# Shifted copies of attention values moved from DMA to VectorE, a split transpose and a gated load

## The chip, the cores and the metric

The kernel runs on one core of a Trainium2 chip. The metric is the device time of one execution in microseconds (us). The engines are TensorE (PE, with its weight loads shown apart as PEld), VectorE (DVE), ScalarE (ACT), GpSimd (POOL) and SyncE (SP); each runs its own instructions in order, and they wait for one another by semaphores. DMAs are issued here from GpSimd's queue and from SyncE's.

## The reference

Eight batches of causal sliding-window attention with eight heads of 576 rows and 64 columns, followed by a two-layer network with SiLU on the 4608 rows of 512 that come out.

```python
rel = pos[:, None] - pos[None, :]
mask_plain = (rel >= 0) & (rel < 32)                         # heads 0 to 3
mask_dil = (rel >= 0) & (rel < 128) & (rel % 4 == 0)         # heads 4 to 7
scores = where(mask, q @ k.T / 8, -1e9)
attn_out = softmax(scores) @ v
x = attn_out.transpose(0, 2, 1, 3).reshape(4608, 512)
h = x @ w_in                                                 # 512 -> 2048
out = (h * sigmoid(h)) @ w_out                               # 2048 -> 512
```

## The kernel before

**The main loop.** For each batch `b`, layer one makes sixteen blocks `h` of 128 hidden features (L700, 8 matmuls with 288 columns each; batch 0 in halves at L720), and ScalarE writes SiLU of them to `gT` (L708). Layer two (L765; batch 0 at L739) multiplies four row tiles of 128 in an even batch and five in an odd one, sixteen matmuls of 512 columns to a tile; `store` copies a finished tile to `ob` (L749, mostly VectorE) and writes it out from SyncE (L750).

**The attention of later batches is laid between.** `plan_of(b)` is a schedule by hand: `at(step, function, ...)` puts a function ahead of a step. Steps 0 to 15 are the sixteen blocks of layer one, and from step 16 on each step is four matmuls of layer two. What stands first in a step is issued first; nothing reorders the instructions of an engine afterwards. `z` is 0 for the four plain heads and 1 for the four dilated ones. `scores` (L371 plain, L383 dilated) are small matmuls, then VectorE adds the mask and takes row maxima (L495, L504, L511), ScalarE takes exponentials (`exps`, L534 and L543), VectorE normalises (`normal`, L552 to L559, writes `pn`), `pn` is turned to `ptT` by TensorE (`turn`, L568, with copies L576) or from batch 2's schedule on by a DMA on SyncE (`turn_by_dma`, L583), and `values` (L610, L674) multiplies with the values, and VectorE and ScalarE copy the result to `xT` (`finish`, L679 to L687).

**The values and their shifted copies.** A query block of 32 rows needs 64 rows of keys and values. `load_v` brings a batch's values from DRAM by six DMAs on GpSimd's queue into `vw`, of which there are two (batch `b` uses `vws[b % 2]`): most go to partitions 64 to 127, blocks of 64 rows. Blocks that start 32 rows later are made from these by four copies inside `vw` to partitions 0 to 63: `shift_class` (L202, 32 partitions x 2048 elements), `shift_over` (L207, 32x1024) and `shift_plain` (L195, 32x2304, and L197, 32x4x512); `shift_v` calls all of them. The argument `copy` says who does it: `nc.sync.dma_start`, `nc.gpsimd.dma_start` or `dve`, which is `nc.vector.tensor_copy`. For batches 2 and 3 the copies are DMAs in GpSimd's queue, for batches 1 and 4 to 7 DMAs in SyncE's; parts of batch 0's are made by VectorE.

**Queries and keys.** From batch 3 on, `load_rows` (L133 for plain heads, L140 for dilated) brings keys, then queries, to `nat` by twelve DMAs on GpSimd's queue, and `cross` turns them on SyncE: `z == 0` by one DMA transpose of 64 partitions x 5120 columns into `plain`, keys in the first half and queries in the second (L150), `z == 1` by two into `strided` (L155, L156). `scores` read `plain` and `strided`.

**What sets the order around the change.** GpSimd's and SyncE's queues are in order, so a DMA that waits for its data holds up all behind it. Before batch 3's `load_v`, GpSimd's queue holds batch 2's four shift DMAs, which wait for batch 2's values to land. In the schedules of `b` = 2 to 5, SyncE's queue holds the four shift DMAs of batch `b + 2` ahead of the two `cross`. A DMA on GpSimd's queue also waits for the one eight ahead of it, since eight semaphores take turns.

Of the kernel before, what the change touches and what calls it, by code (L numbers as in the profile page):

```python
# [8 lines left out]
F16 = mybir.dt.float16  # L9
# [6 lines left out]
P = 128  # L16
W = 32
# [8 lines left out]
RT = 64  # L26
# [3 lines left out]
def kernel(  # L30
# [9 lines left out]
    nc = tc.nc  # L40
    B, H, S, D = q.shape
# [7 lines left out]
    NM = NB // 2  # L49
# [11 lines left out]
    cpool = ctx.enter_context(tc.tile_pool(name="const", bufs=1))  # L61
# [19 lines left out]

    ZR = S // RT + 1
    ZC = W + CL + TL
    natural = [cpool.tile([P, 4 * ZR * P + 2 * HH * DIL * D], F16, name=f"nat{i}") for i in range(2)]
    plain = [cpool.tile([P, W + 4 * ZR * RT], F16, name=f"plain{i}") for i in range(2)]
    strided = [cpool.tile([P, W + 4 * HH * ZC], F16, name=f"strided{i}") for i in range(2)]
    kTs, qTs = [
        [t[:, o : o + 2 * ZR * RT].rearrange("p (i c) -> p i c", i=2)[:, :, 0:n] for t in plain]  # L90
        for o, n in ((0, W + S), (W + 2 * ZR * RT, S))
    ]
# [5 lines left out]
    def natural_of(n, which):  # L98
        o = which * (2 * ZR * P + HH * DIL * D)
        return natural[n % 2][:, o : o + H * 7 * D].rearrange("p (u d) -> p u d", d=D)  # L100
# [21 lines left out]
    def load_rows(b, zs=(0, 1)):  # L122

        n = natural[(b + 1) % 2]
        o = 4 * ZR * P
        f = n[0:RT, 0:o].rearrange("p (x m h d) -> p x m h d", x=4, h=2, d=D)
# [18 lines left out]
    def cross(b, z):  # L145

        n = natural[(b + 1) % 2]
        o, w = 4 * ZR * P, 2 * HH * DIL * D
        if z == 0:
            nc.sync.dma_start_transpose(  # L150
                out=plain[b % 2][:, W:].rearrange("d (g p) -> d g p", p=RT), in_=n[0:RT, 0:o]
            )
        else:
            t = strided[b % 2][:, W:].rearrange("d (g c) -> d g c", c=ZC)
            nc.sync.dma_start_transpose(out=t[:, :, 0:P], in_=n[:, o : o + w])  # L155
            nc.sync.dma_start_transpose(out=t[:, :, P:CL], in_=n[RT : RT + CL - P, 0:w])  # L156
# [82 lines left out]
    def clear_v(b, engine):  # L239
# [13 lines left out]
        out=band[0:W], in_=band[0:W], compare_op=ALU.is_ge, fill=NEG,  # L253
# [3 lines left out]
        out=band[0:W], in_=band[0:W], compare_op=ALU.is_ge, fill=NEG,  # L257
# [471 lines left out]
    dve, act = both = (nc.vector.tensor_copy, nc.scalar.copy)  # L729
# [48 lines left out]
    def transposes(at, b, z, step):  # L778
        for which in (1, 0):
            at(step, transpose, b, z, which, both)  # L780

    def later(at, b, z, steps, copies=(nc.vector.tensor_copy, nc.vector.tensor_copy)):

        for hi in (0, 1):
            if steps[hi] is not None:
                at(steps[hi], normal, b, z, hi)
        for hi in (0, 1):
            at(steps[2], turn, b, z, hi)
        for hi in (0, 1):
            at(steps[2], turned, b, z, hi, copies[hi])  # L790
        at(steps[3], values, b, z)
        at(steps[3], finish, b, z, copies)

    def plan_of(b):
        ev = {}

        def at(s, fn, *args):
            ev.setdefault(s, []).append((fn, args))

        def all_exps(b, z):  # L800
            for hi in (0, 1):
                at(16, exps, b, z, hi)

        if b == 0:

            at(-16, normal, 0, 1, 1)
            at(-15, shift_class, 0, dve, 1, 2)
            at(-14, normal, 0, 0, 1)
            at(-13, clear_v, 1, nc.vector)
            at(-13, load_v, 1)  # L810
            for c in (2, 3):
                at(-13, load_w_out, c)
            at(-13, load_qk, 2)
            at(-8, turn, 0, 1, 1)
            at(-8, turned, 0, 1, 1, act)
            at(-6, values0, 1, 1)
            at(-6, last_values, 0, 1, (1,))
            at(-6, finish0, 1, 1)
            at(-6, last_finish, 0, 1, 1)
            at(-4, turn, 0, 0, 1)  # L820
            at(-4, turned, 0, 0, 1)
            at(-2, values0, 0, 1)
            at(-2, last_values, 0, 0, (1,))
            at(-2, finish0, 0, 1, both)
            at(-2, last_finish, 0, 0, 1)
            transposes(at, 1, 1, 2)
            at(8, scores, 1, 1)
            for hi in (0, 1):
                at(8, shift, 1, 1, hi)
            for which in (1, 0):  # L830
                at(17, transpose, 1, 0, which, (dve, dve))
            at(20, normal, 1, 1, 0)
            at(20, scores, 1, 0)
            at(14, shift_v, 1, nc.sync.dma_start)
            at(17, load_rows, 3)
            at(17, load_v, 2)
            at(17, shift_v, 2, nc.gpsimd.dma_start)
            all_exps(1, 1)
            for hi in (0, 1):
                at(20, exps, 1, 0, hi)  # L840
            for n, z, hi in ((20, 1, 1), (26, 0, 0), (28, 0, 1)):
                at(n, normal, 1, z, hi)
            for n, z, copies in ((27, 1, (dve, dve)), (30, 0, both)):
                for hi in (0, 1):
                    at(n, turn, 1, z, hi)
                for hi in (0, 1):
                    at(n, turned, 1, z, hi, copies[hi])
                at(n + 1 + z, values, 1, z)
                at(n + 1 + z, finish, 1, z, both)
        elif b == 1:  # L850
            transposes(at, 2, 0, 2)
            transposes(at, 2, 1, 11)
            at(2, cross, 3, 0)
            at(20, cross, 3, 1)
            at(28, cross, 4, 0)
            at(8, scores, 2, 0)
            for hi in (0, 1):
                at(8, shift, 2, 0, hi)
            at(17, load_v, 3)
            at(17, load_rows, 4)  # L860
            at(17, shift_v, 3, nc.gpsimd.dma_start)
            at(14, scores, 2, 1)
            all_exps(2, 0)
            all_exps(2, 1)
            for hi in (0, 1):
                at(21, normal, 2, 0, hi)
            at(21, scores, 3, 0)
            at(21, exps, 3, 0, 0)
            at(21, exps, 3, 0, 1)
            later(at, 2, 0, (None, None, 27, 28))  # L870
            later(at, 2, 1, (29, 31, 33, 34))
        else:
            if b + 2 < B:
                at(0, load_v, b + 2)
                if b + 3 < B:
                    at(0, load_rows, b + 3, (1, 0))
                at(8, shift_v, b + 2, nc.sync.dma_start)
                if b + 3 < B:
                    at(12, cross, b + 3, 0)
                at(12, cross, b + 2, 1)  # L880
            if b + 1 < B:
                if b == 2:
                    later(at, 3, 0, (0, 0, 4, 6))
                else:
                    at(6, values, b + 1, 0)
                    at(6, finish, b + 1, 0)
                at(11, scores, b + 1, 1)
                at(11, shift, b + 1, 1, 1)
                all_exps(b + 1, 1)
            if b + 2 < B:  # L890
                at(17, scores, b + 2, 0)
                for hi in (0, 1):
                    at(18, exps, b + 2, 0, hi)
            if b + 1 < B:
                for hi in (0, 1):
                    at(22 + hi, normal, b + 1, 1, hi)
                    at(22 + hi, turn_by_dma, b + 1, 1, hi)
                at(29, values, b + 1, 1)
                at(29, finish, b + 1, 1)
            if b + 2 < B:  # L900
                for hi in (0, 1):
                    at(27 + hi, normal, b + 2, 0, hi)
                    at(27 + hi, turn_by_dma, b + 2, 0, hi)

        def plan(s):
            for fn, args in ev.pop(s, ()):
                fn(*args)

        return plan
# [58 lines left out]
    for b in range(B):  # L968
        plan = plan_of(b)
        if b == 0:  # L970
            for x in range(NFF):
                plan(2 * x - NFF)
                plan(2 * x + 1 - NFF)
                layer1_part(2 * x % NFF, 2 * x // NFF, None if x else warm)
        else:
            for f in range(NFF):
                plan(f)
                layer1(b, f)
        if b == 0:
            layer2_first(plan)  # L980
        else:
            layer2(b, plan)
        for s in range(NFF, 3 * NFF):
            plan(s)
# [30 lines left out]
```

## Time and profile before

| | |
|---|---|
| three runs | 315.63, 312.38, 312.86 us |
| their median | 312.86 us |
| the profiled execution | 314.03 us |
| its span, first to last instruction | 312.1 us |
| granted TensorE clock | 1.00 |
| DMA moved | 41.59 MB |
| shift DMAs of one batch | 128 + 64 + 144 + 128 KB |

The page of the profile names a group of instructions by its line in the kernel, its engine and operation, `out<-in`, a count, the busy time, the mean duration and the idle time of the engine ahead of it with what ended it. In a timeline a row is a start, a duration, and in square brackets the idle time before it and its releaser; "issue" means that the engine waited for nothing that the profile shows. The DMA view shows the packets of each queue in a window and the share of the sixteen DMA engines' time that they took (queueing lets it pass 100%): `q0` holds the DMAs issued from GpSimd, `q1` those from SyncE, `q8` blocks of instructions.

### The profile page before, as it was taken

Reading aid. Unit: us, or ns where it says so; the run is one execution under the profiler, and the core shown is the slowest. Engines: PE = TensorE matmul, PEld = TensorE weight load, DVE = VectorE, ACT = ScalarE, POOL = GpSimd, SP = SyncE. Lnnn points to the kernel's source line nnn. Section 1 sums busy time; section 2 is a strip of 40 time slices with the busy share of each in tenths; the row PEclk is TensorE's granted clock in tenths of the full one; section 3 lists DMA queues with packets and bytes.
Section 4 is the critical chain, followed back from the end, with each engine's and each line's share of the span. In section 5 each row is a group of like instructions: output and inputs, shape, how many; then the busy total and the mean of one; then the engine's idle time right before and its main releaser. Section 6 shows DMA issues by size and latency. Waiting matters only on the chain.

```text
span 312.1 us, 10351 instructions
## 1 busy us (share of the span) xinstructions
PE 298.7 (96%) x4465; PEld 191.7 (61%) x4465; DVE 167.1 (54%) x352; ACT 186.3 (60%) x554; POOL 95.0 (30%) x146
## 2 busy tenths in 40 slices
PE   5899999999999899999999999999999999999995
PEld 2658754677555676467644776467744786467544
DVE  5897588626697436841587036851596034520011
ACT  1776657765993548936595457956695458336300
POOL 8535455823964461075104630040000000000000
PEclk9999999999999999999999999999999999999999
DMA  8999999999999999889987997399115100310022
GB/s 101 176 213 203 185 218 191 169 185 129 144 156 215 153 216 88 205 160 199 110 165 173 182 180 149 92 169 170 27 57 130 65 4 0 114 65 2 0 101 69
DMA packets 105934, 41.59 MB, mean 133 GB/s; under 512 B 79728, under 2 KB 100592, under 8 KB 105888
## 3 DMA queue, kind: packets, MB, share of 16 engines
q0 software_dynamic: 63456, 19.83, 61.1%
q1 hardware_dynamic: 42288, 21.03, 30.6%
q8 instruction: 35, 0.57, 0.8%
q14 instruction: 11, 0.09, 0.1%
q10 hardware_dynamic: 144, 0.07, 0.1%
HBM read 37.75 MB, written 9.44 MB: 151 GB/s over the span
## 4 chain that ended last, share of the span: by engine, by line
PE 89%; DVE 4%; ACT 3%; issue 2%; DMA 1%; POOL 1%; POOLq 0%; DVEq 0%
PE h L700 36%; PE o L765 33%; PE o L739 5%; PE h L720 4%; PE x L610 3%; PE s L383 2%; PE s L371 1%; PE t L321 1%; PE pt L568 1%; DMA ptT<-pn 1%; ACT pe L543 1%; PE x L636 1%; PE xs L674 1%; DVE ms L468 0%; DVE pn L559 0%
## 5 line engine op out<-in xcount | busy, mean ns | idle before, releaser
L708 ACT ACTIVATE gT<-h 128x576 f16<-128x576 f32 x112 | 73.0, 651 | 83.2 <-PE h L700 83.0
L765 PE MATMUL o<-w_out,gT 128*128 128x512 f16 (+1 forms) x528 | 114.1, 373 | 0.0
L700 PE MATMUL h<-xT,w_in 128*128 128x288 f16 x896 | 113.5, 286 | 0.0
L700 PEld LDWEIGHTS <-w_in 128*128 128x128 f16 x896 | 86.4, 98 | 23.3 <-DVE xT L687 0.3
L765 PEld LDWEIGHTS <-gT 128*128 128x128 f16 x528 | 50.6, 98 | 54.9
L543 ACT ACTIVATE pe<-ms,nm 128x64 f32<-128x64 f32 x178 | 59.1, 333 | 4.2 <-DVE nm L511 4.2
L749 DVE COPY ob<-o 128x512 f32<-128x512 f32 (+1 forms) x34 | 23.1, 680 | 49.8 <-PE o L765 49.1
L495 DVE SCALAR_TENSOR_TENSOR ms<-s,mask 128x512 f32<-128x512 f32 x28 | 19.2, 685 | 42.8 <-PE s L383 26.8
L543 ACT ACTIVATION_READ_ACCUMULATOR pe<-ms,nm 128x1 f32 x178 | 33.2, 187 | 0.0
L687 DVE CAST xT<-x 128x512 f16<-128x512 f32 x26 | 16.8, 684 | 29.3 <-PE xs L674 29.3
L174 POOL DMA_DIRECT2D vw<-in_v_dram x16 | 10.1, 638 | 58.8 <-PE xs L674 57.9
L559 DVE TENSOR_TENSOR pn<-pe,r 128x640 f16<-128x640 f32 (+2 forms) x32 | 25.3, 792 | 1.1
L511 DVE TENSOR_REDUCE nm<-ms 128x10 f32<-128x640 f32 (+1 forms) x28 | 22.0, 786 | 1.0
L720 PE MATMUL h<-xT,w_in 128*128 128x256 f16 (+1 forms) x128 | 18.3, 299 | 0.1
L133 POOL DMA_DIRECT2D nat<-in_k_dram x20 | 14.9, 761 | 5.8 <-DMA vw<-in_v_dram 5.1
L133 POOL DMA_DIRECT2D nat<-in_q_dram x20 | 14.7, 760 | 5.6 <-DMA nat<-in_k_dram 3.0
L720 PEld LDWEIGHTS <-w_in 128*128 128x128 f16 x128 | 12.8, 103 | 4.5 <-issue 0.8
L739 PE MATMUL o<-w_out,gT 128*128 128x512 f16 x64 | 15.0, 380 | 0.0
L727 ACT ACTIVATE gT<-h 128x512 f16<-128x512 f32 (+1 forms) x16 | 10.4, 651 | 6.9 <-PE h L720 6.7
L610 PEld LDWEIGHTS <-vw 64*64 64x64 f16 x896 | 8.8, 108 | 7.9 <-issue 7.9
L610 PE MATMUL x<-ptT,vw 64*64 64x32 f16 x896 | 10.5, 187 | 2.6 <-issue 1.3
L749 ACT COPY ob_last<-o 128x128 f32<-128x128 f32 x1 | 0.3, 266 | 17.0 <-DVE ob_last L749 17.0
(102 smaller groups left out, 252.4 us busy)
## 6 DMA issues: line engine op xcount, KB each, us to landing
out_dram<-ob SPq DMA_DIRECT2D x35, 256.0 KB, 3.9
vw<-in_v_dram POOLq DMA_DIRECT2D x8, 288.0 KB, 7.9
vw<-in_v_dram POOLq DMA_DIRECT2D x16, 128.0 KB, 6.3
w_in<-in_moe_w_in_dram POOLq DMA_DIRECT2D x4, 512.0 KB, 12.4
w_out<-in_moe_w_out_dram POOLq DMA_DIRECT2D x4, 512.0 KB, 10.8
nat<-in_k_dram POOLq DMA_DIRECT2D x6, 256.0 KB, 8.1
nat<-in_q_dram POOLq DMA_DIRECT2D x6, 256.0 KB, 9.1
nat<-in_k_dram POOLq DMA_DIRECT2D x20, 72.0 KB, 7.7
```

The source lines that it names most:

```text
L133: nc.gpsimd.dma_start(out=f[:, 2 * (1 - which) + h // 2, 0 : ZR - 1, h % 2], in_=src[b, h].rearrange("(m p) d -> p m d", p=RT),)
L495: nc.vector.scalar_tensor_tensor(out=ms[:, 0:8].rearrange("p (n t) c -> p n (t c)", n=2), in0=s[hi].rearrange("p n t c -> p n (t c)"), sca ...
L511: nc.vector.tensor_reduce(out=nm[:, 0:w], in_=ms[:, 0:w], axis=AX.X, op=ALU.max, negate=True)
L543: nc.scalar.activation(pe[:, t, :], slot(t), AF.Exp, scale=1.0 if b else scale, bias=nm[:, t : t + 1], accum_out=l[:, t : t + 1],)
L559: nc.vector.tensor_tensor(pn[:, 0:w], a["pe", z, hi][:, 0:w], r[:, 0:w, None].broadcast_to([P, w, KB]), ALU.mult)
L610: nc.tensor.matmul(dst, w, p, start=True, stop=True)
L700: nc.tensor.matmul(h[:, half, 0:HS], w_in16[:, c, f * P : f * P + P], xT[:, c, half * HS : half * HS + HS], start=(c == 0), stop=(c == MC ...
L708: nc.scalar.activation(gT[:, f, s0 : s0 + S].rearrange("p (a c) -> p a c", a=2), h[:, :, 0:HS], AF.Silu)
L720: nc.tensor.matmul(h[:, i, 0 : c1 - c0], w_in16[:, c, (f + i) * P : (f + i + 1) * P], xT[:, c, c0:c1], start=(c == 0), stop=(c == MC - 1),)
L739: nc.tensor.matmul(o, gT[:, f, t * P : (t + 1) * P], w_out16[:, f, :], start=(f == 0), stop=(f == NFF - 1),)
L749: copy(ob, o)
L765: nc.tensor.matmul(o, gT[:, f, t * P : (t + 1) * P], w_out16[:, f, m0:m1], start=(f == 0), stop=(f == NFF - 1),)
```

## The change

```diff
+    latch = cpool.tile([P, 1], F16, name="latch")
...
         if z == 0:
-            nc.sync.dma_start_transpose(
-                out=plain[b % 2][:, W:].rearrange("d (g p) -> d g p", p=RT), in_=n[0:RT, 0:o]
-            )
+            for c0, c1 in ((0, o // 2), (o // 2, o)):
+                nc.sync.dma_start_transpose(
+                    out=plain[b % 2][:, W + c0 // 2 : W + c1 // 2].rearrange("d (g p) -> d g p", p=RT),
+                    in_=n[0:RT, c0:c1],
+                )
...
             at(17, load_rows, 3)
             at(17, load_v, 2)
-            at(17, shift_v, 2, nc.gpsimd.dma_start)
...
+            at(17, nc.gpsimd.tensor_copy, latch, qTs[1][:, 1, S - 1 : S])
             at(17, load_v, 3)
             at(17, load_rows, 4)
-            at(17, shift_v, 3, nc.gpsimd.dma_start)
+            at(16, shift_v, 2, dve)
...
-                at(8, shift_v, b + 2, nc.sync.dma_start)
...
             if b + 1 < B:
+                at(1 if b == 2 else 0, shift_plain, b + 1, dve, 0, NM)
+                at(12, shift_class, b + 1, dve, 0, 2)
+                at(12, shift_over, b + 1, dve)
```

The shift copies of batches 2 to 7 leave the two DMA queues and become four VectorE copies a batch: batch 2's in the schedule of `b` = 1 at step 16, the first of layer two; for batches 3 to 7 the two plain copies at step 0 of the schedule of the batch before (step 1 for batch 3) and the other two at step 12. The plain transpose of each of batches 3 to 7 becomes two DMAs, keys and then queries, of 64x2560 each. In GpSimd's queue a copy of one column of batch 3's turned queries into `latch` stands ahead of `load_v` of batch 3; `latch` is read by nobody, and the copy waits until the second of the two DMAs of `cross(3, 0)` has landed. The instructions of TensorE and ScalarE and their order stay the same.

## The prediction

> **What bounds the kernel now.** I read the busy table of the page, then TensorE's waits, then its timeline around each wait, then the DMA queues in narrow windows.
>
> ```profile
> PE 298.7 (96%) x4465; PEld 191.7 (61%) x4465; DVE 167.1 (54%) x352; ACT 186.3 (60%) x554; POOL 95.0 (30%) x146
> q8 instruction: 35, 0.57, 0.8%
> ```
>
> TensorE is busy for 298.7 of 312.1 us, so no edit off TensorE can give more than its gaps. The change first acts at 62 us; the waits of TensorE from there on:
>
> ```profile
> PE x L610 <- issue: 1.3, 1, 1.3
> PE s L383 <- issue: 1.2, 2, 0.7
> PE ss L383 <- issue: 0.9, 2, 0.5
> PE x L610 <- DMA ptT<-pn: 0.7, 1, 0.7
> PE x L610 <- DVE ptT L576: 0.6, 2, 0.3
> ```
>
> That is 4.7 us in all, a ceiling of 1.5%. The largest part, 3.4 us, is called "issue": 0.70 us at 75.56, 1.30 at 107.54, 0.48 at 114.83, 0.32 at 149.36 and 0.55 at 186.12. TensorE's timeline shows two of them, with the same place in the schedule of b = 5 last:
>
> ```profile
> 107.05 0.48 PE L610 MATMUL x<-ptT,vw 64*64 64x32 f16 x37
> 108.84 0.40 PE L610 MATMUL x<-ptT,vw 64*64 64x32 f16 x27 [1.30 <-issue]
> 109.06 0.24 PE L674 MATMUL xs<-ptT,vw 64*64 64x32 f16 x8
> 109.23 5.07 PE L700 MATMUL h<-xT,w_in 128*128 128x288 f16 x40
> 114.23 0.59 PE L383 MATMUL s<-strided 64*32 64x64 f16 x53
> 115.31 0.27 PE L383 MATMUL s<-strided 64*32 64x64 f16 x11 [0.48 <-issue]
> ...
> 218.94 0.68 PE L383 MATMUL s<-strided 64*32 64x64 f16 x64
> 219.44 0.32 PE L383 MATMUL ss<-strided 64*32 64x64 f16 x16
> ```
>
> Between the two gaps lie 27 + 8 + 40 + 53 = 128 matmuls, with a weight load each 256 instructions. Counted through the program, all five gaps stand at the same remainder of 256. The page has 35 instruction packets of 0.57 MB, 16 KB each, and TensorE's 8930 instructions over 35 make 255 to a packet. So a gap is TensorE waiting for its next block of instructions. The windows date each block: the packets end at 73.7, 106.3, 112.9, 147.1 and 184.1 us, each about 2.5 us ahead of the end of a gap (76.26, 108.84, 115.31, 149.68, 186.67). The boundary before each gap, where the next block can first be asked for, lies at 68.25, 98.6, 108.84, 143.5 and 180.3: the fetch took 5.4, 7.7, 4.1, 3.6 and 3.8 us. With quiet queues it took 0.8 (219.85 to 220.7), and there is no gap. Where values of plain heads and scores of dilated heads follow each other in layer one, boundaries are only 5.8 us apart; less 2.5, a fetch of up to 3.3 us is free there. What fills the queues then (windows 102:104 and 112:114):
>
> ```profile
> q1 hardware_dynamic: 755, 0.19, 108.8%
> q0 software_dynamic: 17, 0.05, 20.9%
> ...
> q0 software_dynamic: 727, 0.33, 127.6%
> q1 hardware_dynamic: 25, 0.10, 13.4%
> ```
>
> In the first it is the transpose of batch 4's plain q and k, in the second loads from GpSimd.
>
> **Shift DMAs removed.** 464 KB a batch for six batches is 2.8 of 41.6 MB. For batches 2 and 3 they stood in GpSimd's queue, which sat idle 3.8 + 5.4 us for them around 70 and 76 us; batch 3's went out at 93 to 94.5 and landed after 8 to 11 us, beside batch 4's transpose (issued at 93.77 for 8.64 us against 4.2 elsewhere, landing after 15.8 against 6.8 median). The fetch of 7.7 us ran through just that. Without them I expect the transpose near its median: issued about 92, landed about 99 to 100, and the fetch asked for at 98.6 done before 105.0 (107.54 less 2.5). Of the 1.30 us I take 1.0; ends 0 and 1.30.
>
> At 75.56 the fetch fell into batch 3's transpose (q1 at 111% in 70:72) and batch 2's loads (q0 at 342% in 72:74). Two shift DMAs go, the rest stays. It has to come 0.7 us sooner: I take 0.35, half; ends 0 and 0.70.
>
> The other three gaps, 1.35 us in all, need fetches 0.3 to 0.8 us shorter. The shift DMAs lie on q1, which had 66% and 14% in the 4 us of the fetch at b = 2, and 32, 21 and 8% at b = 3, against q0's 80 to 190%. Most of the crowd stays, and without the shifts GpSimd's loads pack closer. I take 0.3; ends 1.35 gained and 5 lost (second rival).
>
> **The turn by DMA.** SyncE was in the transposes of q and k until 129.08 us; `pn` was ready at 127.35 and 129.45, and its two transposes went out from 129.81 to 132.39. TensorE waited for them from 132.86 to 133.60, 0.74 us. Those transposes waited for GpSimd's loads, the last issued at 118.46. In 104 to 116 us GpSimd lost 2.1 us to shift DMAs whose semaphore it needed, and SyncE's four shifts shared the DMA engines. With loads 1 to 2 us sooner, and keys turned while queries still land, SyncE is free about 127, and landing moves up by the 0.9 us needed: 0.74 gained, ends 0 and 0.74. At b = 3 and 4 there is no wait here.
>
> **The split.** A DMA of 40 blocks costs SyncE 4.2 us, the smallest transposes in the trace 1.2. Two halves cost 4.2 to 5.4 in sum, and I take 4.4, from the row of the same shape. SyncE waits for output tiles anyway (91.8 us in all); cover gone, 1.2 us would hit only `turn_by_dma` at b = 2.
>
> **VectorE.** It made the same copies for batch 0:
>
> ```profile
> 16.72 0.42 DVE L202 COPY vw<-vw 32x1024 f16<-32x1024 f16 x1
> 17.06 0.41 DVE L195 COPY vw<-vw 32x1024 f16<-32x1024 f16 x1
> 17.50 0.35 DVE L197 COPY vw<-vw 32x768 f16<-32x768 f16 x1
> ...
> 17.01 0.58 POOL L117 DMA_DIRECT2D nat<-in_k_dram  x1 [2.00 <-DMA w_in<-in_moe_w_in_dram]
> ```
>
> 256 elements more cost 0.065 us, so 2048 take 0.68 and 2304 take 0.74; a batch costs 0.68 + 0.42 + 0.74 + 0.68 = 2.5 us, about 2.3 with the overlap of starts. Batch 2's four start when VectorE has made its maxima (80.3) and end at 82.6 to 82.8; the next copy, `ob`, waited for TensorE until 82.62. Behind it VectorE is busy without a break up to `ptT` at 91.5, for which TensorE waits 0.58 us, so any overrun is paid: 0 to 0.3, I take 0. Batch 3's plain pair follows `normal` at 104.1, ends about 105.4, and moves `ptT` from 105.7 to 106.2, needed at 107.05: 0. For batches 4 to 7 the pair falls into idle time (137.9 to 143.7 at b = 3). The other pair, 1.0 us at step 12, falls into idle times of 2.4 to 2.9 us ahead of L495: 0.
>
> The last row above is GpSimd issuing a DMA while VectorE copied: 0.58 us, as in its other rows, so I charge GpSimd nothing. [...]
>
> **The gate.** The latch itself is a tiny instruction (128x1 on GpSimd: 0.10 us). Behind it wait batch 3's and 4's loads. The transposes it waits for were issued at 62.80 and their packets stop about 72, so it opens at 72 to 74, where the loads started at 77.66. If they landed after 15.8 us, the worst row, it opens at 78.6, 0.9 later; batch 4's transpose is not needed before 121 us: 0.
>
> **Sum.** 1.0 + 0.35 + 0.3 + 0.74 = 2.4 us, so 314.03 becomes 311.6. The profiled execution lies 1.2 above the median of the runs, so there 312.86 becomes 310.5.
>
> **Rivals.**
> *Everything clears (25%).* All 3.4 us of fetch gaps and the 0.74 go: 4.1, so 308.8. For it: fetches of 3.6 to 4.1 us need to lose little. Against: q0 stays.
> *Only the turn gains (22%).* The edits do not reach the fetches, or the gaps are no fetches: 0.74, so 312.1. Against the second: the remainder of 256. [...]
> *Fetches get later (8%).* Loads no longer held up by shifts pack into b = 2 to 4. If the three short fetches take 5.4 us, as at 68.25, each gap is 5.4 + 2.5 - 5.8 = 2.1, 6.3 in sum against 1.35: 5 lost, 2.1 gained elsewhere, so 315.8; and 316.5 without the turn's gain. It loses from about 1.1 us more per fetch on. For it: q0 beyond 150% at b = 3. Against: fewer bytes in all.
> *My sum (45%)*, 309.7 to 311.5.
>
> **Numbers.** 310.5. From 309.0 to 312.8 leaves out half of the first rival and the third, 2 in 10. One per cent, what I take as the least that a measurement tells from no change, is 3.1 us: faster has the first rival and an edge of the sum, 0.27; slower most of the third, 0.07; the same, 0.66.
>
> **What would show it.** After 62 us TensorE's issue gaps fall from 3.4 to about 1.7 us; the gap inside L610 at b = 2 (107.5) nearly goes; the DMA wait at 133 goes, with the turns issued by 128; VectorE gains 24 copies and about 15 us and TensorE no new wait on it; GpSimd starts batch 3's values at 72 to 74. It is wrong if gaps move to other boundaries, or if `ob` or `ptT` at b = 1 come later.

## The result and the profile after

| | before | after |
|---|---|---|
| median of 22 runs each | 313.03 us | 316.02 us |
| lowest to highest | 311.37 to 317.06 | 312.98 to 317.62 |
| ratio, 95% interval | | 1.0086 (1.006 to 1.0113) |
| profiled execution, its span | 314.03, 312.1 us | 315.12, 313.2 us |
| granted TensorE clock | 1.000 | 0.994 |

The change makes the kernel 0.9% slower; 0.75% faster was forecast. Here and below a ratio leaves out runs more than 1.5% above the fastest of the same kernel (two of before here) and is not the quotient of the medians, which would be 1.0096. The two profiled executions hide the loss: that of before lies 1.0 us above its median, that of after 0.9 below. From the first matmul of layer one of b = 1 (at 59.02 and 60.05 us) to the end they take 253.1 and 253.2 us.

The busy table and the DMA line of the kernel after:

```profile
PE 299.7 (96%) x4465; PEld 192.1 (61%) x4465; DVE 183.5 (59%) x376; ACT 186.5 (60%) x554; POOL 92.4 (30%) x139
DMA packets 104590, 38.74 MB, mean 124 GB/s; under 512 B 79504, under 2 KB 99856, under 8 KB 104544
```

VectorE has its 24 copies more, and 2.85 MB have left the DMA queues. TensorE's waits after 62 us (total, times, longest):

```profile
PE x L613 <- DVE ptT L579: 2.2, 2, 2.0
PE s L386 <- issue: 0.8, 1, 0.8
PE ss L386 <- issue: 0.4, 1, 0.4
```

The issue gaps fell from 3.4 to 1.2 us and the 0.7 us for turned weights (the `ptT` that a DMA makes from `pn`) are gone, but the wait for VectorE's `ptT` at b = 1 grew from 0.6 to 2.2. TensorE's timeline shows what lies behind that wait:

```profile
90.90 1.03 PE L768 MATMUL o<-w_out,gT 128*128 128x512 f16 x4
93.89 0.17 PE L613 MATMUL x<-ptT,vw 64*64 64x32 f16 x1 [1.97 <-DVE ptT L579]
94.29 1.04 PE L613 MATMUL x<-ptT,vw 64*64 64x32 f16 x63 [0.23 <-DVE ptT L579]
95.12 0.31 PE L677 MATMUL xs<-ptT,vw 64*64 64x32 f16 x8
95.36 5.56 PE L768 MATMUL o<-w_out,gT 128*128 128x512 f16 x20
```

In the kernel before, the same place reads:

```profile
91.14 0.17 PE L610 MATMUL x<-ptT,vw 64*64 64x32 f16 x1 [0.35 <-DVE ptT L576]
91.53 0.68 PE L610 MATMUL x<-ptT,vw 64*64 64x32 f16 x63 [0.23 <-DVE ptT L576]
92.04 0.24 PE L674 MATMUL xs<-ptT,vw 64*64 64x32 f16 x8
92.21 4.49 PE L765 MATMUL o<-w_out,gT 128*128 128x512 f16 x20
```

The 63 + 8 + 20 matmuls take 1.5 us longer after the change. The narrow windows give the reason; the number after POOL's count is the granted clock:

```profile
92.00:93.00 1.00, 0.00 (x0) 0.00 (x0) 0.97 (x3) 1.00 (x8) 0.00 (x0) 1.00 1.98 171
94.00:95.00 1.00, 0.78 (x54) 0.71 (x56) 0.83 (x2) 1.00 (x8) 0.00 (x0) 0.58 1.75 163
95.00:96.00 1.00, 1.00 (x36) 0.61 (x29) 0.67 (x2) 1.00 (x8) 0.00 (x0) 0.50 1.40 214
96.00:97.00 1.00, 1.00 (x3) 0.30 (x2) 0.96 (x6) 1.00 (x8) 0.00 (x0) 0.50 1.19 361
97.00:98.00 1.00, 1.00 (x5) 0.44 (x4) 0.97 (x3) 0.98 (x5) 0.00 (x0) 0.72 1.12 251
```

After the wait the clock is at half for 3.4 us. So a wait that grew by 1.6 us cost 3.1. Why it grew stands on VectorE and on GpSimd beside it:

```profile
81.54 0.87 DVE L205 COPY vw<-vw 32x2048 f16<-32x2048 f16 x1
82.43 0.50 DVE L210 COPY vw<-vw 32x1024 f16<-32x1024 f16 x1
82.97 1.06 DVE L198 COPY vw<-vw 32x2304 f16<-32x2304 f16 x1
84.06 0.77 DVE L200 COPY vw<-vw 32x2048 f16<-32x2048 f16 x1
84.75 0.67 DVE L752 COPY ob<-o 128x512 f32<-128x512 f32 x1
...
93.42 0.81 DVE L579 COPY ptT<-pt 128x512 f16<-128x512 f16 x2
```

```profile
81.76 3.38 POOL L134 DMA_DIRECT2D nat<-in_k_dram  x4
85.13 2.93 POOL L134 DMA_DIRECT2D nat<-in_q_dram  x4
```

In the kernel before, the same two instructions of VectorE were:

```profile
82.62 0.69 DVE L749 COPY ob<-o 128x512 f32<-128x512 f32 x1 [2.25 <-PE o L765]
90.67 0.81 DVE L576 COPY ptT<-pt 128x512 f16<-128x512 f16 x2
```

The four copies sum to 3.2 us rather than 2.5, while GpSimd issues loads; its four instructions beside them take 3.38 us and the next four 2.93. Where GpSimd is quiet the copies of 2048 and 1024 elements take the 0.68 and 0.42 us that were foreseen (at 122 us). This profile runs 1.1 us behind that of before by the time it gets here (the matmuls after the first gap start at 77.39 against 76.26), so, less that, `ob` is 1.0 us late against 82.62 and `ptT` 1.6 against 90.67. The copies overrun the time for which `ob` waited anyway by 1.0, and from `ob` to `ptT` VectorE needs 8.67 us against 8.05.

### The profile page after: what moved, and what is told of

Its sections match the earlier page's. It is cut to its first block, busy times and chain, and to the rows that moved or that the text cites. A ratio compares the mean times of both kernels' runs of the same rounds, so it can differ in the third digit from the quotient of the medians.

```text
span 313.2 us, 10360 instructions
## 1 busy us (share of the span) xinstructions
PE 299.7 (96%) x4465; PEld 192.1 (61%) x4465; DVE 183.5 (59%) x376; ACT 186.5 (60%) x554; POOL 92.4 (30%) x139
## 3 DMA queue, kind: packets, MB, share of 16 engines
q1 hardware_dynamic: 41296, 19.13, 29.0%
## 4 chain that ended last, share of the span: by engine, by line
PE 83%; DVE 6%; ACT 4%; DMA 3%; issue 2%; POOL 1%; POOLq 0%; DVEq 0%; SPq 0%
PE h L703 35%; PE o L768 29%; PE o L742 5%; PE h L723 4%; PE x L613 3%; DMA nat<-in_q_dram 2%; ACT pe L546 2%; PE s L386 1%; PE s L374 1%; DVE pn L562 1%; PE t L324 1%; PE pt L571 1%; DMA ptT<-pn 1%; DVE ms L498 1%; DVE l L555 1%
```

## The experiments

All ratios are to the kernel before, run on the same chip, with their 95% intervals. The line numbers move by a few from kernel to kernel.

**One part at a time.** Four kernels: the changed one with batch 2's copies back in GpSimd's queue; the changed one with them three steps earlier; the one before with only batch 2's part; the one before with only batches 3 to 7.

```diff
 e1: changed kernel
+            at(17, shift_v, 2, nc.gpsimd.dma_start)
-            at(16, shift_v, 2, dve)
 e2: changed kernel
-            at(16, shift_v, 2, dve)
+            at(13, shift_v, 2, dve)
 e3: kernel before, with the latch, the gate and
-            at(17, shift_v, 2, nc.gpsimd.dma_start)
+            at(16, shift_v, 2, dve)
 e4: kernel before, with the three lines of copies at steps 0 (1) and 12, and without
-            at(17, shift_v, 3, nc.gpsimd.dma_start)
-                at(8, shift_v, b + 2, nc.sync.dma_start)
```

> The changed kernel with batch 2's shift copies back as DMAs in GpSimd's queue; copies of batches 3 to 7 by VectorE, the split transposes and the gate stay. Theory A (batch 2's four copies stand ahead of the copy ob on VectorE at step 16 of b = 1, delay ptT, TensorE waits 2.2 us and its clock halves for some 3 us): the wait on ptT at b = 1 is back near 0.6 us, the granted clock is 1.00, and the ratio to the kernel before is 0.990 to 1.000. Rival B (the copies of batches 3 to 7, 13 us of VectorE, cost the time): 1.005 to 1.010. Rival C (the gate or the split costs it): 1.005 to 1.010.

> The changed kernel with batch 2's four VectorE copies at step 13 of b = 1 and not at step 16, so that they stand ahead of the masks of batch 2's dilated scores. Theory A: VectorE idles 2.8 us there, the copies wait for batch 2's plain values until about 76 to 77 us and push the masks back by 0 to 1.5 us, ob is on time again, the wait on ptT falls from 2.2 to about 0.6 to 1.2 us, ratio 0.990 to 1.003. Rivals B and C: as the changed kernel, 1.005 to 1.010.

> The kernel before with only batch 2's copies by VectorE at step 16 of b = 1, and the gate in the place of its DMAs in GpSimd's queue; batches 3 to 7 by DMA and whole transposes as before. Theory A: the wait on ptT at b = 1 is about 2 us, the clock falls to 0.5 after it, ratio 1.007 to 1.013, the whole loss or more. Rival B: 0.998 to 1.002. Rival C: between, 1.003 to 1.008, without the wait on ptT.

> The kernel before with only the copies of batches 3 to 7 by VectorE, in the places of the change; batch 2's by DMA, no gate, no split. Theory A: the gaps in which TensorE waits for instructions from 104 us on get smaller, no new wait, ratio 0.990 to 0.999. Rival B: 1.005 to 1.010. Rival C: 0.990 to 0.999 also.

Measured: e1 1.002 (0.9988 to 1.0053), e2 1.0026 (0.9997 to 1.0055), e3 1.0249 (1.0197 to 1.0301) and e4 0.9957 (0.993 to 0.9984). Batches 3 to 7 gain what was expected of them in e4. Taking batch 2's copies off step 16 wins back about 0.6%, by DMA or at step 13 alike: there TensorE waits 0.9 and 0.7 us for `ptT`, and the clock stays at 1.00. But e3 was twice as bad as any theory had it, and e1, which leaves only the split, the latch and the gate beside the copies of e4, was 0.6% above e4. Something else was in it.

**The clock, the split, the gate.** e5 is the changed kernel with seven matmuls of 512 columns that fill TensorE's wait at b = 1 with work that is overwritten; e6 is e4 with the split, e7 is e4 with the latch and the gate, e8 is the changed kernel without the gate's instruction.

```diff
 e5: in values, where (b, z) == (2, 0)
+            for _ in range(7):
+                nc.tensor.matmul(
+                    x[0].rearrange("p n (a c) -> p (n a) c", c=P), ident,
+                    ident[:, None, :].broadcast_to([P, 4, P]), start=True, stop=True,
+                )
 e8: changed kernel
-            at(17, nc.gpsimd.tensor_copy, latch, qTs[1][:, 1, S - 1 : S])
```

> The changed kernel with seven matmuls of 512 columns more, ahead of batch 2's plain values, into the tile that those values overwrite; the results are the same. They fall into the 2 us in which TensorE waits for ptT at b = 1. If the lost clock behind that wait follows from the idle time (theory A's second half): the wait stays but is filled, the clock stays at 1.0 from 94 to 98 us, the next twenty matmuls of layer two take 4.5 us and not 5.6, and the ratio falls by some 0.3 to 0.5% to 1.003 to 1.006. Rival: the clock falls for another reason, and the ratio stays at 1.007 to 1.011.

> The kernel before with the copies of batches 3 to 7 by VectorE and the plain transposes in two halves; batch 2's copies by DMA, no gate. Against batches 3 to 7 alone (0.9957): if the split costs what is missing between that and the changed kernel with batch 2 by DMA (1.002), 1.000 to 1.004; if it costs nothing or helps the keys start early, 0.992 to 0.998.

> The kernel before with the copies of batches 3 to 7 by VectorE and the gate ahead of batch 3's values; batch 2's copies by DMA, whole transposes. If the gate costs what is missing (GpSimd's loads for batches 3 and 4 wait for a transpose that lands at 77 us): 1.000 to 1.004; if not, 0.993 to 0.998, with batch 3's loads at about 78 us in both.

> The changed kernel without the gate: batch 3's loads go out from 65 us on, beside batch 3's transpose. Theory A: the wait on ptT at b = 1 stays near 2 us or a little shorter, since GpSimd is done issuing earlier and stretches VectorE less, ratio 1.004 to 1.009. If the gate itself costs much: below 1.003. If the gate protects the transpose and the instruction blocks: scores of batch 3 wait at 85 us, ratio above 1.010.

Measured: e5 1.0025 (0.9991 to 1.0059), e6 0.9941 (0.9908 to 0.9974), e7 1.0024 (0.9986 to 1.0062) and e8 1.0036 (0.9997 to 1.0076). In e5 the values still start only when `ptT` is there (93.66 us), but TensorE is busy until 0.31 us before:

```profile
91.68 1.67 PE L598 MATMUL x<-ident 128*128 128x512 f16 x7
93.66 0.17 PE L619 MATMUL x<-ptT,vw 64*64 64x32 f16 x1 [0.31 <-DVE ptT L579]
94.74 4.49 PE L774 MATMUL o<-w_out,gT 128*128 128x512 f16 x20
```

The clock stays at 1.00 there and the kernel is 0.6% faster than the changed one: the halved clock, not only the wait, is dear. The split costs nothing. With the gate e4's gain was gone, though the gate did not even wait there. In e7's GpSimd timeline its row has no idle time ahead of it, since batch 2's shift DMAs stand ahead of it:

```profile
77.68 0.59 POOL L198 DMA_DIRECT2D vw<-vw  x1
78.26 0.20 POOL L910 COPY latch<-plain 128x1 f16<-128x1 f16 x1
78.38 1.25 POOL L175 DMA_DIRECT2D vw<-in_v_dram  x2
```

Without the gate (e8) batch 3's values load from 65.36 us on, and the issue gap at b = 1 grows to 2.77 us, but the wait for `ptT` falls to 1.2: the gate moves a loss more than it makes one. (The profiled execution of e8 is its slowest, 1.7 us above its median.)

**A latch that waits for nothing.** e9 and e10 are e4 and e7 once more, e11 has the latch copy a constant column, and e12 is meant to keep all gains: e4 with the split and batch 2's copies at step 13, without latch or gate.

```diff
 e11: as e10, but
-            at(17, nc.gpsimd.tensor_copy, latch, qTs[1][:, 1, S - 1 : S])
+            at(17, nc.gpsimd.tensor_copy, latch, ident[:, 0:1])
```

> The kernel before with the copies of batches 3 to 7 by VectorE and nothing else, once more, as the base that the two kernels with a latch are read against on the same chip. Both theories: 0.993 to 0.9985 of before, as in its first run; no wait of TensorE on the turned weights at 132 us, SyncE issuing the turns by 127.5.

> The same and the gate, once more. Theory (the gate delays batch 3's values and so the loads of batches 4 and 5 behind them): 1.000 to 1.005 of before, 0.4% or more above the kernel without the gate on this chip; a wait of 1 us or more on the turned weights of batch 2 again. Rival (the first difference was a matter of chip and chance): within 0.2% of the kernel without the gate, and no such wait.

> The same with a latch that copies a constant column, so that GpSimd makes the instruction at the same place but waits for no transpose. The loads of batch 3's values stay behind batch 2's shift DMAs as in the kernel without a latch. Theory (it is the gate's wait): as the kernel without a latch, 0.993 to 0.9985 of before. Rival (any GpSimd instruction there costs it): as the kernel with the gate, 1.000 to 1.005.

> All copies of batches 2 to 7 by VectorE, batch 2's four at step 13 rather than 16, the whole-batch transpose split, and no gate. If the gate and the place of batch 2's copies are what the change lost, this keeps its gains and pays neither: 0.992 to 0.997 of before, no wait of more than 1 us of TensorE on ptT at 92 us and the granted clock full there. If batch 3's loads, which can now start at 65 us beside batch 2's transpose, need the gate, TensorE's issue gaps at 76 to 82 us sum to 2 us or more, as in the kernel without the gate, and it is 1.000 to 1.004.

Measured: e9 0.9953 (0.9923 to 0.9982), e10 1.0049 (1.0014 to 1.0085), e11 1.0069 (1.0041 to 1.0097) and e12 0.9984 (0.9945 to 1.0023). The theory that the gate's wait costs it fell: a latch that waits for nothing costs as much as the gate. It is not the wait, and 0.2 us of GpSimd ahead of loads that are early can hardly be 1%. The queue table has the clue. Queue q1 of e9 and then of e11, packets, MB and share of the span:

```profile
q1 hardware_dynamic: 41136, 19.13, 26.8%
```

```profile
q1 hardware_dynamic: 41136, 19.13, 30.4%
```

The same packets and bytes keep the engines busy a seventh longer. The turned weights, which late in the kernel move through quiet queues (the DMA engines are 0.18 and 0.20 busy from 255 to 275 us), land there after 2.4 and 2.6 us. The median landing of the value loads of 128 KB is 4.5 and 6.7. Of the kernels that move these 19.13 MB, all with the latch's *tile*, e8 without its instruction among them, have 29.0% or more and 2.6 us; all without it have at most 27.1% and 2.4. The tile is allocated ahead of the buffers. In the compiled programs its 2 bytes a partition take 32 and move all that follow:

```
first byte in a partition     before    after
latch                              -    89344
nat0                           89344    89376
plain0                        118016   118048
vw0                           140800   140832
pn (first)                    191744   191776
ptT (first)                   197888   197920
ob (first)                    213248   213280
```

89344 is 349 x 256. Before, `nat`, `vw`, `pn`, `ptT` and `ob` stood on multiples of 256 bytes; now none does. (`plain1` and the two `strided` did not before either.)

**The buffers' place.** e13 is the whole change with a latch of 256 bytes, which leaves every buffer where it was against 256; e14 is the kernel before with an unused tile of 2 bytes and nothing else; e15 is e13 with `[P, 32]`, 64 bytes; e16 is e13 with batch 2's copies at step 13. e17 and e18 are e10 and e3 with 256 bytes.

```diff
 e13
-    latch = cpool.tile([P, 1], F16, name="latch")
+    latch = cpool.tile([P, 128], F16, name="latch")
-            at(17, nc.gpsimd.tensor_copy, latch, qTs[1][:, 1, S - 1 : S])
+            at(17, nc.gpsimd.tensor_copy, latch[:, 0:1], qTs[1][:, 1, S - 1 : S])
 e14: kernel before
+    pad = cpool.tile([P, 1], F16, name="pad")
```

> The changed kernel whole, gate and all, but the latch's tile is 256 bytes wide instead of 2 (32 taken), so every buffer behind it stands as it did before against multiples of 256 bytes. Theory A (the 32 bytes are the cost): about 0.8% under the changed kernel, 0.996 to 1.004 of before; q1 busy for 26 to 28% of the span rather than 29.0; the turned weights land after 2.4 us in the median rather than 2.6. Rival (the gate or its instruction costs it): 1.006 to 1.011 as the changed kernel, q1 at 29% or more.

> The kernel before and a tile of 2 bytes that nothing uses, where the change allocates the latch: 32 bytes more ahead of all buffers, not one instruction more. Theory A: 1.004 to 1.012, more rather than less since the shift DMAs write these buffers too; q1 above 32% of the span against 30.6; the turned weights after 2.6 us. Rival: 0.998 to 1.002 and q1 at 30 to 31%.

> The changed kernel with a latch of 64 bytes: the buffers lie on multiples of 64 again, but q's and k's loads, the values and the weights no longer on multiples of 256. If 64 is what counts, as the kernel with 256 bytes, 0.996 to 1.004 and q1 at 26 to 28%. If 256 is what counts, as the changed kernel, 1.005 to 1.011 and q1 at 29% or more. Either is told by q1's share even where the times overlap.

> The changed kernel with the latch of 256 bytes and batch 2's four copies at step 13 instead of 16. If the 32 bytes and the place of these copies are the two losses and add up, 0.6 to 0.7% under the one with 256 bytes alone, so 0.990 to 0.998 of before; no wait on ptT over 1 us at 92 us, no drop of the granted clock there. If batch 2's copies cost only where the buffers are moved, it is within 0.2% of the one with 256 bytes alone.

> Batches 3 to 7 by VectorE and the gate, with a latch of 256 bytes. If all that the gate seemed to cost was the 32 bytes: 0.992 to 0.9985 of before, as the kernel without a gate, and no wait of TensorE on the turned weights of batch 2. If the gate costs something by itself: 1.000 or more.

> The kernel before with batch 2's copies by VectorE at step 16 and the gate, with a latch of 256 bytes; batches 3 to 7 by DMA. If the 32 bytes were 2 to 3% of the kernel with the shift DMAs, as in e14, this comes out at 0.998 to 1.007: batch 2's copies cost 0.6 to 0.8% by the wait and the clock behind it, less what their two GpSimd DMAs gave back. If batch 2's copies by themselves are that dear, 1.02 or more. The wait on ptT at 92 us is 1.5 us or more in either case.

| | ratio | interval | q1 | turned weights |
|---|---|---|---|---|
| e13, whole change, 256 bytes | 1.0035 | 1.0005 to 1.0065 | 26.3% | 2.4 us |
| e14, before, 32 bytes | 1.0281 | 1.0234 to 1.0329 | 32.3% | 2.6 us |
| e15, whole change, 64 bytes | 1.0107 | 1.0067 to 1.0147 | 29.7% | 2.6 us |
| e16, e13 with step 13 | 0.9954 | 0.9933 to 0.9975 | 27.3% | 2.4 us |
| e17, e10 with 256 bytes | 0.9945 | 0.9913 to 0.9977 | 26.6% | 2.4 us |
| e18, e3 with 256 bytes | 1.0039 | 1.0007 to 1.0072 | 28.8% | 2.4 us |

e14 settles it: not one instruction differs from the kernel before, and 32 bytes make it 2.8% slower, more than was expected. TensorE's waits after 62 us:

```profile
PE x L611 <- DMA ptT<-pn: 4.4, 3, 2.3
PE x L611 <- issue: 2.2, 2, 1.2
PE s L384 <- issue: 2.1, 2, 1.6
PE ss L384 <- issue: 1.5, 1, 1.5
PE x L611 <- DVE ptT L577: 0.6, 2, 0.4
```

The issue gaps rise from 3.4 to 5.8 us and the waits for turned weights from 0.7 to 4.4, 3.4 of it in two waits at b = 2, behind which the clock halves too. All waits together are 10.8 us against 4.7; these 6.1 us and the 1.7 lost in 3.4 us at half the clock make 7.8 of the 8.8 us by which this execution's span is longer. A row of the windows there:

```profile
139.00:140.00 1.00, 1.00 (x79) 0.99 (x74) 0.09 (x1) 0.00 (x0) 0.21 (x1) 0.50 0.99 254
```

With 256 bytes the gate costs nothing (e17 against e10, a difference of 1.0%), and e3's excess is gone (e18 against e3, 2.1%). In the whole change the 32 bytes cost some 0.5% (1.0086 against 1.0035), with intervals that just touch; with batch 2's copies at step 13 they cost 0.7%, with intervals apart (e2 against e16). 64 bytes do not help (e15 against e13, on one chip), so multiples of 64 are not what counts; 128 bytes were not tried. How the 32 bytes lengthen the transfers of q1 was not shown, and which of the moved buffers matters most was not tried.

The split has a part here that e6 alone does not show. Of the kernels with the 32 bytes, those with whole transposes (e3, e7, e10, e11, e14) wait 1.6 to 4.4 us for turned weights after 62 us, and those with the split (the changed one, e1, e2, e5, e8) not at all.

What is left is batch 2's place: e13 to e16, 0.8%, on one chip and with intervals apart. In e13's profile, which is of its slowest run (316.12 us against a median of 313.71), the clock's part is larger than in that of after:

```profile
94.22 0.18 PE L613 MATMUL x<-ptT,vw 64*64 64x32 f16 x1 [1.99 <-DVE ptT L579]
94.62 1.04 PE L613 MATMUL x<-ptT,vw 64*64 64x32 f16 x63 [0.22 <-DVE ptT L579]
95.45 0.31 PE L677 MATMUL xs<-ptT,vw 64*64 64x32 f16 x8
95.69 7.12 PE L768 MATMUL o<-w_out,gT 128*128 128x512 f16 x20
```

Against 0.68, 0.24 and 4.49 that is 3.1 us, where after's profile had 1.5. At step 13 the same place reads:

```profile
93.07 0.17 PE L613 MATMUL x<-ptT,vw 64*64 64x32 f16 x1 [0.91 <-DVE ptT L579]
93.47 0.68 PE L613 MATMUL x<-ptT,vw 64*64 64x32 f16 x63 [0.22 <-DVE ptT L579]
93.97 0.24 PE L677 MATMUL xs<-ptT,vw 64*64 64x32 f16 x8
94.15 4.49 PE L768 MATMUL o<-w_out,gT 128*128 128x512 f16 x20
```

The mean clock of every run bears this out. One stretch of 3.41 us at half the clock lowers the mean over 313 us to 0.995, two to 0.989. Of the 22 runs of the changed kernel 11 have 0.989 to 0.995, with a median of 316.1 us, and the eight at 0.999 or 1.00 have 314.3. Of the twelve runs each of e1 (by DMA), e5 (wait filled) and e16 (step 13) none has a mean between 0.985 and 0.996. Means of 0.976 to 0.984 I take for 10 to 14 us at half the clock early in the kernel, where the change does not act: the profile of e2 (0.977) has it at 0.50 from about 10 us on, that of e9 (0.978) lowers it between 8 and 23 us. At 0.976 to 0.978 a later stretch can hide in them (e9), which leaves three runs of e1 and three of the changed kernel open.

The ledger: the copies of batches 3 to 7 alone give -0.4 to -0.5%, and adding the split, the gate and batch 2 at step 13 changes nothing that can be measured (e16, -0.46%). From there step 16 adds 0.81 and the 32 bytes 0.51, which make +0.86% because they are steps of one chain; taken in the other order, by e2, the 32 bytes add 0.72 and step 16 adds 0.60. e4, e6, e9, e16 and e17 all beat both kernels, by 0.4 to 0.6% and 1.3 to 1.4% (quotients of the ratios), and their order among themselves is open. So is whether the gate helps where buffers stand well: e12, without it, has 0.9984 (0.9945 to 1.0023) against e16's 0.9954, but seven of e12's twelve runs have a mean clock of 0.971 to 0.973 or 0.993 to 0.995 and none of e16's, and its profile is not of such a run.

## Why the prediction was wrong

**Right.** The issue gaps are fetches of instructions, as far as counting shows it: in fifteen traces (before, after, e1 to e9, e11, e13, e14 and e16) the 40 issue gaps of 0.3 us or more that were counted after 62 us all stand at the same remainder of 128 matmuls, to within one record. In the kernel after 1.2 us are left where about 1.7 were forecast, with the gap inside L610 at 107.5 gone. The terms of that sum came out less well: the gap at 75.56 grew from 0.70 to 0.83 us where 0.35 were to be gained, and the three short ones shrank by 0.97 in sum where 0.3 were forecast, so that the total came out near is in part luck.

By one execution each, the gaps sum to 2.2 to 5.8 us in the four kernels that keep the shift DMAs of batches 3 to 7 and to 0.2 to 2.9 in the others, with 4.7 in e8; in the first group they rise with q1's share (28.8 to 32.3%), in the second they do not (0.2 us at 30.5% in e5, 2.8 at 26.8% in e12). The view counts a packet where it begins, so the dates that the prediction calls ends of the blocks are beginnings; each block took 0.9 to 1.2 us more and ended about 1.5 us ahead of the end of its gap, which leaves the sums as they are. Of the 35 blocks in the kernel before, five left a gap after 62 us. Thirty of the 35 begin 0.2 to 7.8 us behind the boundary at which the prediction has them asked for, and five begin 0.6 to 2.9 us ahead of it: that a block can first be asked for there was my estimate.

The wait for the turned weights went, in the kernel after although it issues them at 129.72 and not by 128, since TensorE is itself later there; in e4 they go out at 127.17. The split costs nothing. In the kernel after, copies of batches 3 to 7 took 0.68, 0.42, 0.75 and 0.76 us and hold nobody up. What the sum had as a gain, 2.4 us, came out at about 1.3 to 1.8 (0.4 to 0.6% of 313); e4's profile keeps 2.2 us of issue gaps, where 1.7 were forecast.

**The step that failed by its bound** is VectorE's: "any overrun is paid: 0 to 0.3, I take 0". The rule was right and its size wrong. I took the copies at 2.5 us, from rows beside which GpSimd issued a single DMA (17.01), ended them at 82.6 to 82.8, and put no row of GpSimd's from there beside them, although the loads of batch 4 stand there in the trace of before as well (81.62 to 89.58). They took 3.2 us, the next instruction, `ob`, was 1.0 us late, `ptT` 1.6: the sign that the prediction itself had named. What the two do to each other I had looked for on GpSimd's side only, by the one row of 0.58 us, and charged nothing: here its instructions stretch by 0.4 us in four (3.38 against 2.93), and VectorE's copies by a quarter (3.2 against 2.5). That GpSimd's issuing is what stretched them is read from rows and no run isolates it: with the gate and the copies at step 16 the four need 3.2 to 3.5 us (the changed kernel, e3, e13), at step 13, where GpSimd issues beside the last two alone, 2.5 and 2.7 (e2, e16). The other 0.6 us lie between `ob` and `ptT`, 0.5 of it in two small instructions (L559 after, L556 before: 0.42 and 0.51 us against 0.17 and 0.24). The copies did not slow those, since e9, whose batch 2 is copied by DMA, has 0.51 and 0.51; what did was not separated.

**The step that was missing** behind it: a longer wait of TensorE was priced at its own length. With the clock halved after it, 1.6 us became 3.1 in one execution and 4.7 in another, and the copies' place cost 0.8% over all runs of e13 and e16. The clock did not fall each time: in the profiled executions of e3 and e18 the wait is 1.99 and 1.90 us, and the clock after it is 1.00.

**The step that failed without a sign in the trace** is the gate: "The latch itself is a tiny instruction ... 0". Its instruction and its wait do cost nothing, although it opened at 77.25 and not at 72 to 74. What cost 0.5% (0.7% with the copies at step 13) was the tile's declaration, the first line of the diff, which I had not costed at all. No rival had it.

## What to carry to other kernels

A new tile can cost by where it pushes the others, 0.5 to 2.8% here: allocate small tiles last, or round them up to 256 bytes, and look at a queue's busy share per byte when two kernels with the same DMAs differ. A wait added to TensorE is to be priced with the clock that may follow it, one to three times its growth here, so a copy that just fills a hole ahead of a busy stretch belongs elsewhere; here three steps earlier was enough. Time an instruction by rows in which its neighbours on other engines do what they will do in its new place.

## What the runs showed of the hardware

- 32 bytes of offset raised q1's busy time for the same 19.13 MB from 26.3 to 27.3% of the span (seven kernels) to 29.0 to 31.1% (eight), and a kernel that moves 41.6 MB lost 2.8% by it.
- After 62 us the clock fell to 0.50 behind single waits of TensorE of 2.0 us (after, e13) and 2.5 (e9, an issue gap), and behind two waits in a row of 2.3 and 1.2 (e14) and of 0.5 and 1.2 (e3). It stayed there for 3.4 us each time (3.41 in after), and twice that in e13. It did not fall behind single waits of 2.0 (e3) and 1.9 (e18) for `ptT`, nor behind two in a row of 0.6 and 1.2 (e7), and in e8 a gap of 2.77 left it at 1.00:

```profile
78.48 0.20 PE L386 MATMUL s<-strided 64*32 64x64 f16 x1
81.45 0.67 PE L386 MATMUL s<-strided 64*32 64x64 f16 x63 [2.77 <-issue]
81.94 0.32 PE L386 MATMUL ss<-strided 64*32 64x64 f16 x16
```

  So 2.0 us sufficed, and not always. What decides was not tried.
- Beside GpSimd's issuing of `nat` loads at 82 us VectorE's copies of 32 partitions took 0.87 us rather than 0.68, 0.50 rather than 0.42 and 1.06 rather than 0.75 (the fourth 0.77, as elsewhere), and the four issues 3.38 us rather than 2.9 to 3.0. Beside the next batch's loads at 108 us two copies took 0.75 and 0.76, as elsewhere, and GpSimd's two issues 1.79 rather than 1.32 to 1.34 (all in the kernel after). Which side is slowed was not separated.
